# Opening the first MoE chunk half way through batch 0, and dividing attention outputs by the row sum instead of the probabilities

## The chip, the cores and the metric

The kernel runs on one core of a Trainium2 chip. The core has TensorE (PE in the profile: matmuls and transposes, with weight loads in a row of their own, PEld), VectorE (DVE), ScalarE (ACT), GpSimd (POOL) and SyncE (SP), which here only issues DMAs. Each engine works through its own list of instructions in a fixed order; a waiting instruction holds back everything behind it on that engine. The metric is the device time of the whole program in microseconds.

## The reference

Three stages in fp32, the output of each feeding the next. What matters here:

```
scores   s = scale * q_l k^T          # window of +-32 keys and 32 global keys; 4 batches x 8 heads x 512 queries, D = 64
p        e = exp(s - max(s));  p = e / (sum(e) + 1e-9)
out      o = p v                       # plus 32 global queries per batch that see all keys
x        = o of all heads side by side # 4 x 544 tokens, 512 wide
moe 1    h = x w_in;  g = max(h, 0) + alpha * min(h, 0);  x = g w_out      # w_in 512 x 2048, w_out 2048 x 512
moe 2    logits = x w_gate; every token goes to one of 8 experts of equal capacity; out = relu(x w1[e]) w2[e]
```

The weights of moe 1 and w_gate come as float64 and are decoded on the core.

## The kernel before

A tile scheduler writes the instruction lists: the kernel issues operations in an order of its own, and the scheduler, led by its own timeline, reorders them on each engine before the lists are fixed.

**Attention.** The work is cut into 16 units `u` = (batch, pair of heads), four to a batch, and each unit into two halves `j` of 256 queries (two blocks of 128). A *unit half* is the piece that the text counts in. For each, `scores` does four matmuls into PSUM, a fused mask-and-minimum on DVE (L376) and an exponential with row sums on ACT (L378); `norm` adds 1e-9 to the sums, takes the reciprocal (L384, L385) and multiplies the four 128x224 tiles of probabilities (L393 on DVE; with the flag `share` set, every second one on ACT, L391); `ptrans` transposes them on PE in two parts (L402), each copied to SBUF by ACT (L404); `pv` multiplies with v on PE (L413), and ACT copies the 128x256 result into `xb` (L414), the transposed activations of the batch. Per pair of units there is also a global part: `gscores` (L425, L427, L431), `gnorm`, `gtrans` (L450, L444) and `gpv` (L462), whose DVE copy (L465) fills the first 32 columns of `xb`. `gout` writes finished units to memory.

The generator `attention` runs the unit halves in the order (0,0), (0,1), (1,0), (1,1), ...: scores of number n, norm and transposes of n-1, pv of n-2. Loads are issued two units ahead (`load`, 736 KB of q and k, three buffers; `load_v`, 512 KB, four buffers).

**First stage, attention alone.** While `alone[0]` is set, PSUM is split among tags: `s` tiles have four banks, transposes two (`pX`), and everything else (`gs`, `gt`, `go`, `o`) shares the two banks of `pY`. The loop `while done[0] < UPB - 1` runs the generator until batch 0 has been written out, and decodes up to four parts of `w_in`. `decode` is one ACT operation (L78), four DVE operations on 128x512 (L79, L81, L82, L83), a cast on ACT (L67) and a subtraction on POOL (L68).

**Second stage, attention beside MoE.** Then a pool of four banks serves all attention tiles, and `gemm(c, 0)` starts: chunk `c` has 272 tokens, half a batch. `splitx` splits `xb` into a rounded part xh (ACT) and a rest xl (DVE L68, 128x1088). `gemm1` does twelve 128x272 matmuls (L167) for each of eight column blocks, DVE evaluates the activation from PSUM (L172, L186), ACT and POOL split it (`ghi`, `glo`), and the second product takes 96 matmuls (L200). A ratio of 0.9 shares turns between attention and MoE. The other twelve weight parts are decoded here, one per MoE step; `tc.issue_after(at_norm[UPB - 1, 1].ins)` puts their DVE work behind the last normalization of batch 0. `share` stays set until the parts are used up.

**Later stages.** Once attention is over, the second halves of `w_in` and `w_out` are decoded under the remaining chunks; then come the second half of moe 1, the router and the experts.

Of the kernel before, what the change touches and what calls it, by code (L numbers as in the profile page):

```python
# [15 lines left out]
OP = mybir.AluOpType  # L16
# [9 lines left out]
def tile_attention_moe_moe(ctx: ExitStack, tc: tile.TileContext, qkw, vw,  # L26
# [277 lines left out]
    with ExitStack() as at:  # L304
        mk = at.enter_context(tc.tile_pool(name="mk", bufs=1, side="right"))
        ld = at.enter_context(tc.tile_pool(name="ld", bufs=3, side="right"))
# [23 lines left out]
        NU = len(units)  # L330
        U = [dict() for _ in units]
# [14 lines left out]
        def load_v(u):  # L346
            d = U[u]
            vv = ld.tile([128, 2, NB, 2 * D], F32, name="vv", bufs=4)
            nc.sync.dma_start(out=vv.rearrange("p a i d -> p (a i d)"), in_=vw[u])
            d["va"], d["vb"] = vv[:, 0], vv[:96, 1]  # L350
# [5 lines left out]
        def scores(u, j):  # L356
            d = U[u]
            if j == 0:
# [4 lines left out]
                d["pr"] = pp.tile([128, 2, NB, KW], F32, name="pr")  # L363
                d["sm"] = pp.tile([128, 2, NB], F32, name="sm")
                d["mx"] = pp.tile([128, 2, NB], F32, name="mx")
# [5 lines left out]
            for ii in range(2):  # L371
                i = 2 * j + ii
                m = mask[:, 0 if i == 0 else 2 if i == NB - 1 else 1]
                for h in range(2):
                    sc = pp.tile([128, KW], F32, name="sc", bufs=4)
                    V.tensor_tensor_reduce(out=sc, in0=s[h][:, ii], in1=m, scale=-D ** -0.5, scalar=BIG,  # L376
                                           op0=OP.add, op1=OP.min, accum_out=d["mx"][:, h, i:i + 1])
                    A.activation(out=d["pr"][:, h, i], in_=sc, func=AF.Exp, bias=d["mx"][:, h, i:i + 1], scale=-1.0,  # L378
                                 accum_out=d["sm"][:, h, i:i + 1])

        def norm(u, j):
            d = U[u]
            sm = d["sm"][:, :, 2 * j:2 * j + 2]
            V.tensor_scalar(sm, sm, 1e-9, None, op0=OP.add)  # L384
            V.reciprocal(sm, sm)  # L385
            for ii in range(2):
                i = 2 * j + ii
                for h in range(2):
                    p, r = d["pr"][:, h, i], d["sm"][:, h, i:i + 1]
                    if h and share[0]:  # L390
                        A.mul(p, p, r)  # L391
                    else:
                        at_norm[u, j] = V.tensor_scalar(p, p, r, None, op0=OP.mult)  # L393

        def ptrans(u, j, half):
# [3 lines left out]
            for ii in range(2):  # L399
                for h in range(2):  # L400
                    p = d["pr"][:, h, 2 * j + ii]
# [4 lines left out]
        def pv(u, j):  # L406
            d = U[u]
            o = bank([128, 2, 128], "o")
# [5 lines left out]
            A.copy(d["x"][:, SG + 256 * j:SG + 256 * j + 256], o.rearrange("p i t -> p (i t)"))  # L414
# [61 lines left out]
        share, at_norm = [False], {}  # L476

        def attention():
# [7 lines left out]

            for n in range(2 * NU + 2):
                u, j = divmod(n, 2)
                if u < NU:
                    if j == 0 and u + 2 < NU:  # L490
                        load(u + 2)
                        load_v(u + 2)
                    scores(u, j)
                    yield 1.0
# [778 lines left out]
```

## Time and profile before

| | us |
|---|---|
| median of 3 runs | 901.78 (901.72 to 903.84) |
| profiled execution | 902.5 |
| its span | 900.7 |
| start of the first MoE matmul (L167) in the trace | 61.70 |

The profile is of one execution. A row of the page names line, engine, operation, the tile written and the tiles read, then how often it runs. Busy times are unions within a window; a matmul's own duration holds its pipeline latency, so what one costs in a stream is read from start to start. An fp32 matmul that is not a transpose leaves two records in the trace, a transpose or an fp32r matmul one. "PEclk" 1.00 means 2.4 GHz, 0.50 means 1.2 GHz.

### The profile page before, as it was taken

Reading aid. Unit: us, or ns where it says so; the run is one execution under the profiler, and the core shown is the slowest. Engines: PE = TensorE matmul, PEld = TensorE weight load, DVE = VectorE, ACT = ScalarE, POOL = GpSimd, SP = SyncE. Lnnn points to the kernel's source line nnn. Section 1 sums busy time; section 2 is a strip of 40 time slices with the busy share of each in tenths; the row PEclk is TensorE's granted clock in tenths of the full one; section 3 lists DMA queues with packets and bytes.
Section 4 is the critical chain, followed back from the end, with each engine's and each line's share of the span. In section 5 each row is a group of like instructions: output and inputs, shape, how many; then the busy total and the mean of one; then the engine's idle time right before and its main releaser. Section 6 shows DMA issues by size and latency. Waiting matters only on the chain.

```text
span 900.7 us, 18727 instructions
## 1 busy us (share of the span) xinstructions
PE 850.4 (94%) x7168; PEld 775.0 (86%) x7168; DVE 542.4 (60%) x1779; ACT 405.6 (45%) x949; POOL 426.3 (47%) x367
## 2 busy tenths in 40 slices
PE   6989999999998899999999999999899999899996
PEld 3677788888897899999999899999498998899995
DVE  5989946565639983355655756677475776621120
ACT  4977555564544452233333333331244444444531
POOL 1225311111106643355666865652567678778721
PEclk8989899999999999999999999999899999999998
DMA  8575414313035521022220215332455556456510
GB/s 294 174 251 174 130 60 152 96 63 125 32 113 157 169 82 63 25 68 95 67 84 1 76 49 168 118 119 72 119 155 169 158 168 187 145 169 183 169 44 36
DMA packets 50273, 107.66 MB, mean 120 GB/s; under 512 B 6728, under 2 KB 23112, under 8 KB 50184
## 3 DMA queue, kind: packets, MB, share of 16 engines
q1 hardware_dynamic: 47288, 97.56, 35.0%
q0 software_dynamic: 2896, 8.92, 2.7%
q8 instruction: 56, 0.92, 0.4%
q14 instruction: 33, 0.27, 0.1%
HBM read 88.63 MB, written 17.83 MB: 118 GB/s over the span
## 4 chain that ended last, share of the span: by engine, by line
PE 33%; DMA 8%; POOL 7%; issue 5%; ACT 3%; DVE 2%; POOLq 0%; ACTq 0%
PE h L1115 11%; PE h L167 10%; DMA raw<-in_moe_w_dram 7%; POOL m L68 6%; PE h L1005 3%; PE h L989 3%; PE lp L239 3%; ACT m L67 2%; POOL xg L940 1%; PE yt L228 1%; PE y L200 1%; PE pc L829 1%; POOL out_dram L1039 0%; DMA x2d<-yr 0%; PE pa L841 0%
## 5 line engine op out<-in xcount | busy, mean ns | idle before, releaser
L68 POOL TENSOR_TENSOR m<-raw,m 128x1024 fp32r<-128x1024 f32 x64 | 152.8, 2392 | 51.5 <-ACT m L67 51.1
L167 PE MATMUL h<-xh,win 128*128 128x272 f32 x768 | 165.5, 296 | 6.4 <-DVE g L186 5.7
L68 POOL TENSOR_TENSOR glo<-g,ghi 128x272 fp32r<-128x272 f32 x64 | 58.0, 909 | 179.3 <-ACT ghi L67 177.1
L167 PEld LDWEIGHTS h<-xh,win 128*128 128x128 f32 x768 | 126.1, 188 | 14.6 <-DVE g L186 7.5
L200 PE MATMUL y<-ghi,wout 128*128 128x272 f32 x512 | 113.0, 300 | 2.4 <-ACT ghi L67 2.0
L167 PE MATMUL h<-xl,win 128*128 128x272 f32 x384 | 111.3, 291 | 0.3 <-DVE xl L68 0.2
L1115 PE MATMUL h<-gr,wout 128*128 128x272 f32 x768 | 110.8, 295 | 0.4 <-POOL gr L68 0.4
L172 DVE TENSOR_SCALAR nm<-h,al 128x272 f32<-128x272 f32 x128 | 63.4, 496 | 77.0 <-PE h L167 76.2
L989 PE MATMUL h<-xsh,m 128*128 128x272 f32 x512 | 106.3, 297 | 1.1 <-ACT xsh L67 1.1
L67 ACT CAST m<-raw 128x1024 fp32r<-128x1024 f32 x64 | 66.9, 1049 | 82.0 <-DMA raw<-in_moe_w_dram 77.1
L1005 PE MATMUL h<-hh,m 128*128 128x272 f32 x512 | 103.4, 294 | 0.0
L1115 PEld LDWEIGHTS h<-gr,wout 128*128 128x128 f32 x768 | 99.3, 189 | 1.3 <-POOL gr L68 0.7
L200 PEld LDWEIGHTS y<-ghi,wout 128*128 128x128 f32 x512 | 84.8, 191 | 8.0 <-issue 4.0
L989 PEld LDWEIGHTS h<-xsh,m 128*128 128x128 f32 x512 | 83.2, 190 | 1.7 <-ACT xsh L67 1.4
L1005 PEld LDWEIGHTS h<-hh,m 128*128 128x128 f32 x512 | 81.5, 189 | 0.2
L200 PE MATMUL y<-glo,wout 128*128 128x272 f32 x256 | 75.3, 298 | 3.0 <-POOL glo L68 3.0
L1005 PE MATMUL h<-hl,m 128*128 128x272 f32 x256 | 75.7, 296 | 0.0
L989 PE MATMUL h<-xsl,m 128*128 128x272 f32 x256 | 75.2, 294 | 0.2 <-DVE xsl L68 0.2
L167 PEld LDWEIGHTS h<-xl,win 128*128 128x128 f32 x384 | 72.4, 189 | 1.6 <-DVE xl L68 0.7
L378 ACT ACTIVATE pr<-sc,mx 128x224 f32<-128x224 f32 x128 | 60.5, 475 | 23.5 <-DVE mx L376 23.2
L68 POOL TENSOR_TENSOR l<-gb,h 128x272 fp32r<-128x272 f32 x62 | 54.5, 893 | 22.9 <-ACT h L67 20.7
L68 POOL TENSOR_TENSOR gr<-gb,gr 128x272 fp32r<-128x272 f32 x64 | 47.9, 773 | 32.7 <-ACT gr L67 32.5
(233 smaller groups left out, 1737.4 us busy)
## 6 DMA issues: line engine op xcount, KB each, us to landing
raw<-in_moe_w_dram SPq DMA_DIRECT2D x64, 512.0 KB, 3.6
qk<-in_qk_dram SPq DMA_DIRECT2D x15, 736.0 KB, 6.6
vv<-in_v_dram SPq DMA_DIRECT2D x16, 512.0 KB, 5.5
raw<-in_moe_w_in_dram SPq DMA_DIRECT2D x16, 512.0 KB, 4.9
raw<-in_moe_w_out_dram SPq DMA_DIRECT2D x16, 512.0 KB, 3.6
xs<-xb SPq DMA_DIRECT2D x16, 272.0 KB, 4.5
xpart<-xd SPq DMA_DIRECT2D x32, 136.0 KB, 1.8
xb<-xs SPq DMA_DIRECT2D x8, 544.0 KB, 3.8
```

The lines of the kernel that those rows point to most:

```text
L67: a = A.copy(hi, src)
L68: return a, (lo_eng or V).tensor_tensor(lo, src, hi.bitcast(F32), op=OP.subtract)
L167: T.matmul(ps, wi[:, w, k, fs], x[:, k], start=i == 0, stop=i == 3 * KD - 1)
L172: V.tensor_scalar(nm, ps, 0.0, al[:, hf * KH + f:hf * KH + f + 1], op0=OP.min, op1=OP.mult)
L200: T.matmul(ps, wo[:, w, f, ds_], x[:, f], start=i == 0, stop=i == 3 * KH - 1)
L228: T.transpose(t[:, k * 128:(k + 1) * 128], tail["x"][:, k] if q == 2 else xo[:, k, a:b], ident)
L239: T.matmul(lp, w, x, start=first and i == 0, stop=last and i == 1)
L378: A.activation(out=d["pr"][:, h, i], in_=sc, func=AF.Exp, bias=d["mx"][:, h, i:i + 1], scale=-1.0, accum_out=d["sm"][:, h, i:i + 1])
L829: T.matmul(pc.rearrange("p a e -> p (a e)"), g[:, c:c + 2].rearrange("p a j -> p (a j)"), ohw[:, c:c + 2].rearrange("p a e -> p (a e)"), s ...
L989: T.matmul(ps, d["w1"][:, w, kk, fs], x[:, kk], start=i == 0, stop=i == 3 * KD - 1)
L1005: T.matmul(ps, d["w2"][:, w, f, ms], x[:, f], start=i == 0, stop=i == 3 * K3 - 1)
L1115: T.matmul(ps[j], wo[:, w, f, ds_], x, start=f == 0 and a == 0, stop=f == KH - 1 and a == 2)
```

## The change

- Batch 0 is done by halves: (0,0), (1,0), (2,0), (3,0), then (0,1), (1,1), (2,1), (3,1). Batches 1 to 3 keep the old order.
- Chunk 0 needs only the first 32 + 240 columns of `xb`. The first loop now ends after pv of (3,0), and `loadx(0, 0)` no longer waits for the whole batch.
- In batches 0 and 1 (`NBO = 2`) the probabilities are left undivided. `pv` spreads the reciprocal sums over the 64 output rows with four more matmuls against the identity into the second half of a 128x512 PSUM tile; ACT copies them to SBUF (`rs`), and DVE multiplies output by `rs` while it writes `xb`. ACT's old copy into `xb` is gone there. In batches 2 and 3 the division is as before, all of it on DVE; the flag `share` is gone.
- q/k buffers go from three to four. The first four units are loaded at once; later loads are issued when the third user of a buffer has been issued, four units ahead.
- Probabilities, sums and maxima have tiles per unit half.
- The remaining weight parts are put behind DVE's last multiply of the first halves of batch 0.

```diff
-        ld = at.enter_context(tc.tile_pool(name="ld", bufs=3, side="right"))
+        ld = at.enter_context(tc.tile_pool(name="ld", bufs=4, side="right"))
...
+        NBO = 2
...
+            d["pr", j] = pp.tile([128, 2, 2, KW], F32, name="pr", bufs=3)
+            d["sm", j] = pp.tile([128, 2, 2], F32, name="sm", bufs=4)
...
             V.tensor_scalar(sm, sm, 1e-9, None, op0=OP.add)
             V.reciprocal(sm, sm)
+            if units[u][0] < NBO:
+                return
             for ii in range(2):
-                i = 2 * j + ii
                 for h in range(2):
-                    p, r = d["pr"][:, h, i], d["sm"][:, h, i:i + 1]
-                    if h and share[0]:
-                        A.mul(p, p, r)
-                    else:
-                        at_norm[u, j] = V.tensor_scalar(p, p, r, None, op0=OP.mult)
+                    p = d["pr", j][:, h, ii]
+                    V.tensor_scalar(p, p, sm[:, h, ii:ii + 1], None, op0=OP.mult)
...
-            o = bank([128, 2, 128], "o")
+            late = units[u][0] < NBO
+            ot = bank([128, 2, 2, 128] if late else [128, 1, 2, 128], "o")
+            o = ot[:, 0]
+            if late:
+                for ii in range(2):
+                    for h, c in heads(u):
+                        T.matmul(ot[c, 1, ii], d["sm", j][:, h, ii:ii + 1].to_broadcast([128, D]), ident,
+                                 start=True, stop=True)
+                rs = tp.tile([128, 2, 128], F32, name="rs")
+                A.copy(rs, ot[:, 1])
...
-            A.copy(d["x"][:, SG + 256 * j:SG + 256 * j + 256], o.rearrange("p i t -> p (i t)"))
+            x = d["x"][:, SG + 256 * j:SG + 256 * j + 256].rearrange("p (i t) -> p i t", i=2)
+            if late:
+                at_norm[u, j] = V.tensor_tensor(x, o, rs, op=OP.mult)
+            else:
+                A.copy(x, o)
...
+            left[kind, u] = left.get((kind, u), 0) + 1
+            if left[kind, u] == 3 and u + 4 < NU:
+                (load if kind == "qk" else load_v)(u + 4)
...
+            seq = [(u, j) for j in range(2) for u in range(UPB)]
+            seq += [(u, j) for u in range(UPB, NU) for j in range(2)]
...
+                    if v == UPB - 1 and j2 == 0:
+                        quarter[0] = True
...
-        while done[0] < UPB - 1:
+        while not quarter[0]:
...
-            if want < NCH and (want, 0) not in X and done[0] >= (want // CPB + 1) * UPB - 1 and (
+            if want < NCH and (want, 0) not in X and (want == 0 or done[0] >= (want // CPB + 1) * UPB - 1) and (
...
-                        with tc.issue_after(at_norm[UPB - 1, 1].ins):
+                        with tc.issue_after(at_norm[UPB - 1, 0].ins):
```

PE around the opening, before: the last pv and the global pv of batch 0, one unit half of batch 1, then the first MoE matmuls (`h`).

```order
L402 MATMUL t<-ident,pr 128x128 x4
L413 MATMUL o<-pt,vv 64x128 x8
L402 MATMUL t<-ident,pr 96x128 x4
L462 MATMUL go<-gt,vv 64x32 x20
L413 MATMUL o<-pt,vv 64x128 x8
L370 MATMUL s<-qk 128x224 x4
L402 MATMUL t<-ident,pr 128x128 x4
L402 MATMUL t<-ident,pr 96x128 x4
L167 MATMUL h_803<-xh,win 128x272
L167 MATMUL h_855<-xh,win 128x272
L167 MATMUL h_803<-xl,win 128x272
```

PE around the opening, now (`o<-ident,sm` are the new matmuls that spread the reciprocal sums):

```order
L413 MATMUL o<-ident,sm 64x128 x8
L421 MATMUL o<-pt,vv 64x128 x16
L371 MATMUL s<-qk 128x224 x4
L401 MATMUL t<-ident,pr 128x128 x4
L401 MATMUL t<-ident,pr 96x128 x4
L167 MATMUL h_603<-xh,win 128x272
L167 MATMUL h_651<-xh,win 128x272
L413 MATMUL o<-ident,sm 64x128 x4
L371 MATMUL s<-qk 128x224 x4
L401 MATMUL t<-ident,pr 128x128 x3
L421 MATMUL o<-pt,vv 64x128 x6
L167 MATMUL h_603<-xl,win 128x272
```

Ahead of the first `h` now stand 28 score matmuls, 48 transposes, 32 pv matmuls and 16 of the new ones; before, 44, 80, 64 and none. The second halves of batch 0 follow behind and between `h`.

DVE ahead of the split of the first chunk (L68, `xl`), before:

```order
L384 TENSOR_SCALAR sm<-sm 128x2x2
L385 RECIPROCAL sm<-sm 128x2x2
L393 TENSOR_SCALAR pr<-pr,sm 128x224 x2
L79 TENSOR_SCALAR mag<-mag 128x512
L81 TENSOR_SCALAR mag<-mag 128x512
L82 SCALAR_TENSOR_TENSOR mag<-raw,mag 128x512
L465 COPY xb<-go 128x2x32
L83 SCALAR_TENSOR_TENSOR mag<-raw,mag 128x512
L79 TENSOR_SCALAR mag<-mag 128x512
L81 TENSOR_SCALAR mag<-mag 128x512
L68 TENSOR_TENSOR xl<-xb,xh 128x1088
```

DVE, now: the rows that end with the multiplies of the first halves of units 2 and 3 (L424); `xl` follows after two decode pairs and one unit half of masking (L377):

```order
L385 TENSOR_SCALAR sm<-sm 128x4
L83 SCALAR_TENSOR_TENSOR mag<-raw,mag 128x512
L386 RECIPROCAL sm<-sm 128x4
L424 TENSOR_TENSOR xb<-o,rs 128x256
L447 TENSOR_SCALAR gmx<-gmx 128x1
L448 RECIPROCAL gmx<-gmx 128x1
L385 TENSOR_SCALAR sm<-sm 128x4
L449 TENSOR_SCALAR gsc<-gsc,gmx 128x608
L386 RECIPROCAL sm<-sm 128x4
L457 COPY gt<-gt 96x128
L477 COPY xb<-go 128x2x32
L424 TENSOR_TENSOR xb<-o,rs 128x256 x2
```

The multiplications of probabilities (L393) are gone from this place, and four multiplies that read PSUM stand in DVE's list where ACT copied before. Ahead of `xl` DVE's list holds 28 masking operations instead of 44 and no multiplication of probabilities instead of 38; of the decode operations 6, 6, 5 and 4 (in the order L79, L81, L82, L83) instead of 8, 8, 7 and 7.

Further on, the stream of 48 matmuls of L200 that ends chunk 0's second product needs the last decoded part of `w_out`. Ahead of it PE's list holds, before: 64 score matmuls, 120 transposes, 104 pv, 142 `h`, 48 `y`. Now: 54, 96, 80, 144, 48, and 44 of the new ones. DVE's list of masking, decode and MoE operations up to the last decode holds 60 maskings before and 48 now.

SP's list of DMA issues from the start, before:

```order
L340 DMA qk<-in_qk_dram 128x960
L341 DMA qk<-in_qk_dram 128x512
L341 DMA qk<-in_qk_dram 128x1472
L349 DMA vv<-in_v_dram 128x1024 x2
L341 DMA qk<-in_qk_dram 128x1472
L349 DMA vv<-in_v_dram 128x1024 x2
L75 DMA raw<-in_moe_w_in_dram 128x1024 x3
L542 DMA al<-in_moe_alpha_dram 128x16x1
L543 DMA wg<-in_moe_w_gate_dram 128x4x8
L341 DMA qk<-in_qk_dram 128x1472
```

SP's list, now:

```order
L341 DMA qk<-in_qk_dram 128x960
L342 DMA qk<-in_qk_dram 128x512
L342 DMA qk<-in_qk_dram 128x1472
L350 DMA vv<-in_v_dram 128x1024
L342 DMA qk<-in_qk_dram 128x1472
L350 DMA vv<-in_v_dram 128x1024
L342 DMA qk<-in_qk_dram 128x1472
L350 DMA vv<-in_v_dram 128x1024 x2
L75 DMA raw<-in_moe_w_in_dram 128x1024 x3
L584 DMA al<-in_moe_alpha_dram 128x16x1
L585 DMA wg<-in_moe_w_gate_dram 128x4x8
L75 DMA raw<-in_moe_w_in_dram 128x1024
```

One more `qk` load of 736 KB stands ahead of the first `raw` (weights), and the fourth unit's q and k no longer stand behind the 128x4x8 load of the gate weights.

## Rows read from the trace of the kernel before

**Rows 1.** Page, part 1: busy time, share of the span and instructions of each engine

```profile
PE 850.4 (94%) x7168; PEld 775.0 (86%) x7168; DVE 542.4 (60%) x1779; ACT 405.6 (45%) x949; POOL 426.3 (47%) x367
```

**Rows 2.** Timeline of PE: the first MoE matmul

```profile
61.70 0.50 PE L167 MATMUL h<-xh,win 128*128 128x272 f32 x2
```

**Rows 3.** Windows by stage: length, busy us (instructions) per engine, PE clock, DMA share, GB/s

```profile
0.00:61.70 61.70, 47.90 (x403) 33.90 (x403) 48.96 (x188) 44.85 (x133) 12.84 (x25) 0.89 0.70 233
61.70:110.00 48.30, 45.17 (x356) 37.15 (x354) 47.00 (x133) 31.74 (x85) 22.61 (x18) 0.93 0.52 163
110.00:265.00 155.00, 155.00 (x1476) 136.41 (x1474) 85.68 (x332) 82.32 (x249) 19.77 (x24) 1.00 0.27 86
265.00:330.00 65.00, 56.90 (x421) 53.68 (x418) 60.31 (x97) 31.29 (x63) 35.28 (x30) 0.97 0.53 166
```

**Rows 4.** Windows of the first 117 us, by granted clock; columns as in rows 3

```profile
16.00:24.00 8.00, 6.16 (x36) 4.20 (x38) 6.12 (x27) 5.89 (x19) 1.32 (x1) 0.57 0.77 209
24.00:46.00 22.00, 19.04 (x179) 12.72 (x177) 21.55 (x84) 20.00 (x64) 4.19 (x3) 1.00 0.60 185
46.00:61.70 15.70, 13.62 (x146) 11.04 (x146) 13.36 (x38) 12.15 (x30) 3.40 (x3) 0.78 0.62 219
61.70:94.00 32.30, 29.26 (x233) 24.74 (x230) 32.27 (x91) 22.15 (x59) 15.09 (x13) 1.00 0.54 178
94.00:102.00 8.00, 7.91 (x71) 6.26 (x71) 8.00 (x18) 4.81 (x14) 4.81 (x3) 0.58 0.70 190
```

**Rows 5.** Waits of PE, 0 to 62: who, for whom, us, times, longest

```profile
PE s L370 <- DMA qk<-in_qk_dram: 4.5, 1, 4.5
PE s L370 <- DVE mx L376: 2.7, 2, 2.5
```

**Rows 6.** Waits of PE, 61.7 to 117

```profile
PE h L167 <- DVE g L186: 2.8, 2, 1.5
```

**Rows 7.** Timeline of PE from 117.0: start, us, operation, records; a next start ends one

```profile
117.00 0.29 PE L200 MATMUL y<-ghi,wout 128*128 128x272 f32 x1
...
122.92 0.29 PE L200 MATMUL y<-ghi,wout 128*128 128x272 f32 x1
123.13 1.10 PE L413 MATMUL o<-pt,vv 128*64 128x128 f32 x16
124.16 1.03 PE L370 MATMUL s<-qk 64*128 64x224 f32 x8
125.12 0.66 PE L402 MATMUL t<-ident,pr 128*128 128x128 f32 x4
125.53 0.38 PE L167 MATMUL h<-xl,win 128*128 128x272 f32 x1
```

**Rows 8.** Lines of DVE, 0 to 110: shapes, count | busy us, mean ns

```profile
L393 DVE TENSOR_SCALAR pr<-pr,sm 128x224 f32<-128x224 f32 x56 | 20.9, 430 | 0.1
L376 DVE CUSTOM_DVE_ANT_0 sc<-s,mask 128x224 f32<-128x224 f32 x60 | 20.9, 379 | 6.9 <-PE s L370 6.5 <-ACT pr L378 0.2
L82 DVE SCALAR_TENSOR_TENSOR mag<-raw,mag 128x512 int32<-128x512 int32 x16 | 13.2, 827 | 0.1
L83 DVE SCALAR_TENSOR_TENSOR mag<-raw,mag 128x512 int32<-128x512 int32 x16 | 11.9, 741 | 0.0
L81 DVE TENSOR_SCALAR mag<-mag 128x512 int32<-128x512 int32 x16 | 8.8, 558 | 0.1
L79 DVE TENSOR_SCALAR mag<-mag 128x512 f32<-128x512 f32 x16 | 7.6, 479 | 1.8 <-ACT mag L78 1.8
```

**Rows 9.** Lines of DVE by form, whole span: an add with one PSUM operand

```profile
L1128 DVE TENSOR_TENSOR pt<-h,pt 128x272 f32<-128x272 f32 x28 | 12.0, 437 | 3.8 <-PE h L1115 2.3 <-issue 0.4 <-ACT m L67 0.3
```

**Rows 10.** Windows, 8 to 16: columns as in rows 3

```profile
8.00:16.00 8.00, 5.55 (x33) 3.15 (x32) 6.60 (x34) 4.44 (x16) 0.00 (x0) 1.00 1.02 412
```

**Rows 11.** Timeline of ACT from 16: start, us, operation [idle before, releaser]

```profile
16.91 0.66 ACT L78 ACTIVATE mag<-raw 128x512 f32<-128x512 f32 x1 [1.89 <-DMA raw<-in_moe_w_in_dram]
```

**Rows 12.** Source view of line 393: duration ns least/median/most

```profile
L393 DVE TENSOR_SCALAR pr<-pr,sm x124: 321/331/1417, 9.5 to 253.8; 128x224 f32<-128x224 f32 x124
```

More of the change, by code (lines that the diff above doesn't have):

```diff
@@ L347, in load_v @@
             d = U[u]
-            vv = ld.tile([128, 2, NB, 2 * D], F32, name="vv", bufs=4)
+            vv = ld.tile([128, 2, NB, 2 * D], F32, name="vv")
             nc.sync.dma_start(out=vv.rearrange("p a i d -> p (a i d)"), in_=vw[u])
@@ L475, in tile_attention_moe_moe, with free, gs_, gp_ @@
         done = [-1]
-        share, at_norm = [False], {}
+        at_norm = {}
+        left = {}
+        quarter = [False]
+        def free(kind, u, j):
+            if u >= NU:
+                return
+            left[kind, u] = left.get((kind, u), 0) + 1
+            if left[kind, u] == 3 and u + 4 < NU:
+                (load if kind == "qk" else load_v)(u + 4)
+        def gs_(p):
+            gscores(p, 0)
+            gscores(p, 1)
+            free("qk", 2 * p, 2)
+            free("qk", 2 * p + 1, 2)
+        def gp_(p):
+            gpv(p)
+            free("vv", 2 * p, 2)
+            free("vv", 2 * p + 1, 2)
         def attention():
@@ L485, in one @@
                     yield x
+            seq = [(u, j) for j in range(2) for u in range(UPB)]
+            seq += [(u, j) for u in range(UPB, NU) for j in range(2)]
             for n in range(2 * NU + 2):
[L488 to L492, printed above, removed]
+                if n < 2 * NU:
+                    u, j = seq[n]
                     scores(u, j)
+                    free("qk", u, j)
                     yield 1.0
                 if 1 <= n <= 2 * NU:
-                    a_ = divmod(n - 1, 2)
-                    norm(*a_)
-                    ptrans(*a_, 0)
+                    norm(*seq[n - 1])
+                    ptrans(*seq[n - 1], 0)
                     yield 0.45
-                    ptrans(*a_, 1)
+                    ptrans(*seq[n - 1], 1)
                     yield 0.45
                 yield from one()
+                if alone[0]:
+                    yield from one()
                 if n >= 2:
-                    pv(*divmod(n - 2, 2))
+                    v, j2 = seq[n - 2]
+                    pv(v, j2)
+                    free("vv", v, j2)
                     yield 1.0
-                    v, j2 = divmod(n - 2, 2)
+                    if v == UPB - 1 and j2 == 0:
+                        quarter[0] = True
+                        yield 0.1
                     if v % 2 and j2:
@@ L517, in tile_attention_moe_moe @@
         load_v(0)
+        load(2)
         load_v(1)
+        load(3)
+        load_v(2)
+        load_v(3)
         mask = mk.tile([128, 3, KW], F32, name="mask")
@@ L545, in tile_attention_moe_moe @@
         alone[0] = False
-        share[0] = True
         first.close()
```

24 lines of the change are left out of this document (10 added, 14 removed).

## The prediction

> **What bounds the kernel now.** I read the busy line first, then windows by stage, then the stretch that the change touches by clock and by waits. TensorE is busy 850.4 of 900.7 us [rows 1], so the time is PE's work plus what PE loses. The first MoE matmul starts at 61.70 [rows 2]. The stage windows show where PE loses: 13.8 us without work up to 61.7 (61.70 - 47.90), 3.1 from there to 110, none from 110 to 265 (155.00 of 155.00), 8.1 from 265 to 330 [rows 3]. By clock: from 16 to 24 and from 46 to 61.7 the granted clock is 0.57 and 0.78, and again 0.58 from 94 to 102 [rows 4]; matmuls at 1.2 GHz take twice as long, so a stretch of 8 us at 0.58 (16% of it at the upper level) has 6.7 us at 1.2 GHz and loses half of that, 3.4. Before 61.7 the largest waits are for the first load (4.5, not avoidable) and for DVE's masking (2.7) [rows 5]; after it, 2.8 us for DVE's activation of the MoE chunk [rows 6]. In both stretches DVE is the full engine: 21.55 of 22.00 us from 24 to 46, 32.27 of 32.30 from 61.7 to 94, while PE has room [rows 4]. So up to 110 DVE, busy 47.00 of the last 48.30 us, sets the pace; from 110 to 265 PE does, and DVE there is at 85.68 of 155 [rows 3].
>
> **What the change adds.** Sixteen unit halves (batches 0 and 1) get four more matmuls each, 64 in all, of the form 128x64 by 128x128, which is that of pv. Sixteen records of pv (eight matmuls) take 1.03 us from start to start (123.13 to 124.16), 0.129 each [rows 7]: 64 x 0.129 = 8.2 us. Going from MoE to attention costs a little: the last `y` starts at 122.92 and pv at 123.13, 0.21 where 48 matmuls from 117.00 took (122.92 - 117.00) / 47 = 0.126 each, so 0.09 a change [rows 7]; a dozen changes more, an estimate, are 1.0. Nothing hides this where PE is full. Batch 1's half of it falls mostly into such a stretch; batch 0's is counted here too and its cover in the next terms. Bounds: 8.2, if the new groups always stand beside pv, and 16.5 if the two column halves did not run side by side as pv's do; I take 9.2, since the form is the same.
>
> On ACT the copy of `rs` replaces the copy into `xb`, same size, and four divisions go: nothing. On DVE 60 divisions go over the whole run and 16 multiplies with one PSUM operand come, 128x256; the nearest row is an add with one PSUM operand on 128x272, 0.437 us [rows 9]. Loads, stores and weights are as many as before; four units' q, k and v are issued ahead of the weights. One q/k load more, 736 KB at 412 GB/s [rows 10], puts the first weights back by 1.8 us, from 16.91 [rows 11] to about 18.7. That counts, because DVE and ACT have the first decode in their lists after three unit halves and wait there. Later loads are issued up to four units ahead, which I cost at nothing; a late one would cost no more than the 4.5 us of the first [rows 5].
>
> **What opening early gives.** At the first `h`, PE's list has done 16 score matmuls, 32 transposes and 32 pv less, and 16 new ones more. A group of 4 score matmuls takes 0.96 (124.16 to 125.12), four transposes 0.41 [rows 7]: 16 x 0.24 + 32 x 0.103 + 32 x 0.129 - 16 x 0.129 = 3.8 + 3.3 + 4.1 - 2.1 = 9.1 us of work less. So each microsecond by which the opening comes before 61.7 - 9.1 = 52.6 is lost time saved.
>
> When does it open? DVE was busy 48.96 us up to 61.7 [rows 3]. Ahead of the split of the chunk its list now lacks 38 divisions at 20.9 / 56 = 0.37, 16 maskings at 20.9 / 60 = 0.35, and 2 + 2 + 2 + 3 decode operations at 0.48, 0.55, 0.83 and 0.74 [rows 8]: 14.1 + 5.6 + 5.9 = 25.6; four multiplies add 1.7. That leaves 25.1. DVE starts at 6.5, the idle time before its first masking [rows 8]. It reaches the first decode after 12 maskings and some small work (12 x 0.35 + 2 for the global part), waits until 18.7 + 0.66 for ACT's first decode step [rows 11], and has about 19 us left: 38.4. With no other wait the opening is at 39, the lower end. The upper end keeps PE's present share: 47.90 busy in the 57.2 us from 4.5 on; 47.90 - 9.1 = 38.8 busy at that share is 46.4, so 51. I take 43, a third of the way up: in the nearest row, 24 to 46, DVE is full and PE busy 19.04 of 22 [rows 4], so the pace is DVE's, but the output tiles of the first stage pass through two PSUM banks, with PE, ACT and DVE taking turns, and that costs some microseconds. Saved: 52.6 - 43 = 9.6 (13.6 to 1.6).
>
> **The stretch after it.** From 61.7 to 117.0, where the stream of 48 `y` starts [rows 7], PE now loses 2.8 us in waits for DVE [rows 6] and 3.4 at the lower clock, which follows the idle time just before 94 [rows 4]: 6.2. In the new kernel DVE does this stretch without divisions (18 of the 56), with 20 maskings against 16, but with 9 more decode operations moved in from ahead of the opening. So DVE is about as full as it was, and PE has more to do beside it (28 new matmuls, a fuller MoE). PE is then nearer to being the bound, and a late DVE finds other matmuls in PE's list. I take half of the loss, 3.1, as gone; the ends are 0 and 6.2.
>
> After that PE has no idle time until attention ends [rows 3], so what was gained is kept. The window 265 to 330, 8.1 us idle and DVE busy 60.31 of 65 [rows 3], is the decode of the second half of the weights. The MoE has then run beside 28 unit halves instead of 24 and is a little under one chunk further; the chunks that are left still outlast the decode, so this wait stays, neither better nor worse.
>
> **The sum** on the span: +9.2 - 9.6 - 3.1 = -3.5, so 897.2. The profiled execution took 902.5, 1.8 above its span, and 0.7 above the median of 901.78: 901.8 - 3.5 = 898.3.
>
> **A rule that speaks against it.** A division lasts 0.331 us at the median and up to 1.417 [rows 12]; the mean of the first 110 us is 0.430 [rows 8], 0.1 more than undisturbed, 5.5 us over 56. In my sum that goes with the divisions. The Trainium skill (SBUF — State Buffer, section Who interferes with whom) says that DVE and GpSimd share one pair of ports, that scalar operations in the two-port mode and operations with two SBUF inputs compete for it with GpSimd, and that the loser is blocked for the whole instruction. The trace has the spread, but does not say who held the ports. By that rule the delay is GpSimd's to hand out and not the division's own: its subtractions for the weights stay, and the decode operations next in DVE's list would take it. The rule makes a rival of its own, the second below.
>
> **Rivals.** First, DVE's list flows: opening at 39 and no loss behind it. That is 4 us and 3.1 us better, 891. For it speaks that DVE's sum is the smaller one; against it that in the trace no stage of this kind ran without handover losses.
>
> Second, GpSimd's blocking moves to the decode (L81, L82), which already average 0.558 and 0.827 [rows 8]. Then DVE keeps about half of 38 x 0.1 ahead of the opening, 2 us, and the stretch behind it gains nothing: 898.3 + 2 + 3.1 = 903.4, no change.
>
> Third, slower: the output tile waits for DVE. Before, ACT emptied it as soon as pv was done; now it waits its turn in DVE's list, and ahead of the four multiplies stand decode operations of 0.83 and 0.74 [rows 8] and maskings. While the tile waits, one of two banks is held, and the next global scores, their transposes or the next output queue behind it on PE, and everything of PE behind those. At one decode pair (1.6) for four tiles ahead of the opening and half of that for the other four of batch 0, it costs 6.4 + 3.2 = 9.6: 908. It decides from an opening later than 46.5, where the rest gives nothing. For it speaks that ACT was the less loaded one, 22.15 of 32.30 against DVE's 32.27 [rows 4]; against it that later there are four banks and other matmuls between.
>
> That the change would not do what it says is ruled out by the lists, which have `h` after 28 score matmuls.
>
> **Chances.** My forecast 45% (893 to 903 by itself), first rival 17%, second 20%, third 18%. Within 0.3%, 899.1 to 904.5, a measurement of this kernel can't tell from no change. Of the forecast's 45, 27 are faster, 16 the same, 2 slower; the first rival's 17 are faster; of the second, 2 faster, 13 the same, 5 slower; of the third, 1 faster, 2 the same, 15 slower. So 47% faster, 31% the same, 22% slower. The range leaves out a tenth at each side: 890.5 to 907.
>
> **What would show it.** The first `h` near 43 and no earlier than 39; the new matmuls at 0.26 a pair; the first decode step of ACT near 18.7 with a wait for DMA before it; DVE's multiplies near 0.43; PE full from shortly after the opening, with the waits for DVE and the stretch at 0.58 shorter or gone; 110 to the end of attention still without idle time. An opening after 47, or PE waits for L424, make the prediction wrong towards slower; waits of the MoE for L82 or L83, towards no change.

## The result, and the profile after

The changed kernel takes 907.94 us (median of 20 runs, 904.13 to 913.12), the kernel before 902.05 (20 runs, 899.77 to 907.55): a ratio of 1.0059, with a 95% interval of 1.0042 to 1.0077. It is slower by about 5.9 us, where 898.3 was forecast. A second measurement of both (e12 below) gave 1.0065 (1.0042 to 1.0088).

The busy line of the page, against [rows 1]: TensorE has 128 matmul records more (the 64 new matmuls, two records each) and 10.2 us more of busy time; VectorE has 12 us less.

```profile
PE 860.6 (95%) x7296; PEld 783.1 (86%) x7296; DVE 530.4 (58%) x1735; ACT 404.9 (45%) x945; POOL 421.9 (46%) x367
```

The first MoE matmul, against 61.70 in [rows 2], in the timeline of PE:

```profile
48.20 0.52 PE L167 MATMUL h<-xh,win 128*128 128x272 f32 x2
```

So the opening did come early, by 13.5 us. The stage windows, against [rows 3], in the same columns (length, busy us and instructions of PE, PEld, DVE, ACT, POOL, then PE clock, DMA share, GB/s):

```profile
0.00:61.70 61.70, 48.31 (x416) 37.12 (x418) 38.89 (x140) 38.61 (x110) 13.63 (x26) 0.86 0.64 222
61.70:110.00 48.30, 45.97 (x352) 36.97 (x347) 43.96 (x117) 31.85 (x85) 18.38 (x16) 0.96 0.49 159
110.00:265.00 155.00, 155.00 (x1473) 134.76 (x1472) 81.99 (x326) 81.49 (x248) 21.25 (x26) 1.00 0.28 90
265.00:330.00 65.00, 61.06 (x519) 56.15 (x518) 50.14 (x100) 30.23 (x67) 24.41 (x22) 1.00 0.42 129
```

Up to 61.70 VectorE was relieved by 10.07 us, but TensorE is busy there for as long as before, 48.31 us against 47.90. The only window in which TensorE's idle time clearly fell is the last, 3.94 us against 8.10, and that is the one the prediction said would stay. The finer windows, against [rows 4]:

```profile
16.00:24.00 8.00, 5.06 (x34) 3.47 (x33) 5.40 (x23) 6.21 (x19) 0.08 (x1) 0.87 0.63 175
24.00:46.00 22.00, 18.23 (x201) 15.16 (x203) 12.08 (x41) 13.50 (x36) 5.44 (x4) 0.66 0.45 164
46.00:61.70 15.70, 15.13 (x136) 12.34 (x132) 15.02 (x42) 10.88 (x30) 4.18 (x4) 1.00 0.63 212
61.70:94.00 32.30, 29.97 (x227) 23.98 (x222) 32.13 (x81) 21.99 (x56) 14.57 (x13) 0.95 0.66 212
```

From 24 to 46 no engine is full any more: VectorE is busy 12.08 of 22 us, ScalarE 13.50, and TensorE 18.23, at a granted clock of 0.66 (a mix of its 1.2 and 2.4 GHz levels). From 46 on VectorE is full again, 15.02 of 15.70 and 32.13 of 32.30. What VectorE lost in divisions it lost where it then had nothing to do; behind the opening it is as full as before. The timeline of PE from 20 us on (idle time and its releaser in brackets) shows work that waits for other work:

```profile
20.42 1.33 PE L371 MATMUL s<-qk 64*128 64x224 f32 x8 [2.67 <-DVE mx L377]
...
23.91 2.35 PE L474 MATMUL go<-gt,vv 128*64 128x32 f32 x40
26.06 1.10 PE L413 MATMUL o<-ident,sm 128*64 128x128 f32 x8
28.69 1.98 PE L437 MATMUL gs<-qk 128*64 128x512 f32 x4 [1.53 <-DVE xb L477]
30.46 1.88 PE L421 MATMUL o<-pt,vv 128*64 128x128 f32 x16
```

The pv group (L421, x16) takes 1.88 us there and 1.10 in [rows 7]. The wait of 2.67 goes back to the first weights: VectorE's next operation was a step of their decode (L79), which waited for ScalarE's first step (L78), and that one for the weights to land:

```profile
18.60 0.43 DVE L79 TENSOR_SCALAR mag<-mag 128x512 f32<-128x512 f32 x1 [2.76 <-ACT mag L78]
17.91 0.66 ACT L78 ACTIVATE mag<-raw 128x512 f32<-128x512 f32 x1 [1.46 <-DMA raw<-in_moe_w_in_dram]
```

### The profile page after: what moved, and what is told of

Same layout as the page of the kernel before. It is cut to its first block, busy times and chain, and to the rows that moved or that the text cites. A ratio compares the mean times of both kernels' runs of the same rounds, so it can differ in the third digit from the quotient of the medians.

```text
span 908.2 us, 18931 instructions
## 1 busy us (share of the span) xinstructions
PE 860.6 (95%) x7296; PEld 783.1 (86%) x7296; DVE 530.4 (58%) x1735; ACT 404.9 (45%) x945; POOL 421.9 (46%) x367
## 4 chain that ended last, share of the span: by engine, by line
PE 57%; DMA 11%; DVE 10%; issue 9%; POOL 8%; ACT 4%; SPq 1%; POOLq 0%; ACTq 0%; DVEq 0%
PE h L167 17%; PE h L1154 11%; DMA raw<-in_moe_w_dram 9%; PE y L200 8%; POOL m L68 6%; PE o L421 3%; PE s L371 3%; PE lp L239 3%; PE t L401 2%; PE h L1028 2%; DVE mag L82 2%; ACT m L67 2%; DMA raw<-in_moe_w_in_dram 2%; POOL xg L979 2%; PE h L1044 1%
## 5 line engine op out<-in xcount | busy, mean ns | idle before, releaser
L68 POOL TENSOR_TENSOR m<-raw,m 128x1024 fp32r<-128x1024 f32 x64 | 152.7, 2391 | 54.0 <-ACT m L67 53.0
L167 PE MATMUL h<-xh,win 128*128 128x272 f32 x768 | 168.4, 299 | 4.1 <-DVE g L186 3.7
L167 PEld LDWEIGHTS h<-xh,win 128*128 128x128 f32 x768 | 127.3, 190 | 13.8 <-DVE g L186 5.9
L68 POOL TENSOR_TENSOR glo<-g,ghi 128x272 fp32r<-128x272 f32 x64 | 56.4, 884 | 170.5 <-ACT ghi L67 168.0
L200 PE MATMUL y<-ghi,wout 128*128 128x272 f32 x512 | 113.0, 299 | 0.4 <-ACT ghi L67 0.3
L200 PEld LDWEIGHTS y<-ghi,wout 128*128 128x128 f32 x512 | 83.9, 189 | 6.5 <-issue 4.2
L200 PE MATMUL y<-glo,wout 128*128 128x272 f32 x256 | 74.6, 295 | 0.0
L68 POOL TENSOR_TENSOR l<-gb,h 128x272 fp32r<-128x272 f32 x62 | 54.5, 893 | 23.0 <-ACT h L67 20.7
L68 POOL TENSOR_TENSOR gr<-gb,gr 128x272 fp32r<-128x272 f32 x64 | 47.9, 773 | 32.9 <-ACT gr L67 32.8
```

The source lines that it names most:

```text
L68: return a, (lo_eng or V).tensor_tensor(lo, src, hi.bitcast(F32), op=OP.subtract)
L167: T.matmul(ps, wi[:, w, k, fs], x[:, k], start=i == 0, stop=i == 3 * KD - 1)
L200: T.matmul(ps, wo[:, w, f, ds_], x[:, f], start=i == 0, stop=i == 3 * KH - 1)
```

## The experiments

All are measured against the kernel before on the same chip; its median there was 901.65 to 903.15, so ratios are compared, not times, and a range in brackets behind a ratio or a difference is a 95% interval. The lines of code are shortened. Theory A was formed from the profile above: the 64 matmuls cost their full price, and the opening came late because TensorE ran a chain of dependent work at 1.2 GHz. Theory B: VectorE's work sets the pace. Theory C: the two PSUM banks that hold the outputs do.

**Each half of the change alone.** e1 keeps order and opening, e2 scales batch 0 only, e3 keeps only the scaling.

```
e1:  NBO = 2  ->  NBO = 0
e2:  NBO = 2  ->  NBO = 1
e3:  seq = [(u, j) for u in range(NU) for j in range(2)]
     while not quarter[0]  ->  while done[0] < UPB - 1   (the chunk's condition and the global parts' turns as before)
```

> The new order and the early opening stay; the outputs are no longer scaled: in both batches the probabilities are divided on VectorE as before, so the 64 matmuls that spread one over the row sum, their ScalarE copies and the 16 multiplies of the outputs are gone. Theory A (the change pays for the added matmuls on TensorE, and the opening came late because TensorE ran its chain of dependent work at 1.2 GHz): the 64 matmuls go at 0.129 us each, 8.2 us, and the chain to the first MoE matmul loses a link, so 899.5 us (897 to 902), first MoE matmul at 46 to 47.5. Theory B (VectorE is what the new opening is short of): 24 more divisions of 0.43 us lie ahead of the opening, it comes later than 50, and batch 1's 32 come back beside the MoE chunk: 905 us or more.

> Outputs are scaled in batch 0 only; batch 1 is divided on VectorE as before. Theory A: 32 matmuls fewer at 0.129 us, 4.1 us, all after the opening: 903.8 us (902.5 to 905.5), the first MoE matmul unchanged at 48.2. Theory B: batch 1's 32 pairs of divisions, 64 of 0.43 us less 8 multiplies of 0.42 us, 24 us of VectorE, delay TensorE in the stretch of the first chunks: not faster than 907.

> The old order and the old opening after the whole of batch 0; only the scaling of the outputs of batches 0 and 1 stays. Theory A: the added 64 matmuls lie on TensorE's path and VectorE's relief gives back at most the 7.2 us of waits of the first stage: 906 us (902 to 910). Theory B: VectorE set the pace of the first stage, and its 27.5 us less of divisions bring the old opening forward by 5 us or more: 900 us or less.

e1: 908.62, ratio 1.0063 (1.0037 to 1.0088). Theory A missed by 9 us; B was right on the opening, at 53.26, with VectorE full in 24:46:

```profile
24.00:46.00 22.00, 17.06 (x165) 12.68 (x165) 21.10 (x61) 14.13 (x38) 7.60 (x5) 0.66 0.51 163
```

So opening early without the scaling costs 5.7 us (3.3 to 7.9), as much as the whole change.

e2: 906.51, 1.0030 (1.0005 to 1.0054), between the two. (Theory B's 24 us for it count batch 1's 32 divisions twice; by the same working they are 10.4.) e3: 909.80, 1.0077 (1.0051 to 1.0103), as A said: the scaling alone costs 7.0 us (4.6 to 9.3), and VectorE's relief does not bring the old opening forward, which comes at 61.24. But the two halves together cost no more than either, so they aren't independent. e1 also lacks ScalarE's share of the divisions; that was only 4 of 128 in the kernel before, and e13 tries a larger one.

**The stall and the clock.** e4 queues the first decode on ScalarE behind unit 3's exponentials; e6 loads the first weights ahead of two units' values; e7 does e4's edit in the kernel before; e17 fills TensorE's wait with repeated transposes. (e7, and e15 and e16 below, also put the split of the gate weights behind a later exponential.)

```
e4:  with tc.issue_after(last_exp[UPB - 1, 0].ins): f(dc, 0, i)
e6:  load_v(2), load_v(3) issued behind the first and the second part
e7:  with tc.issue_after(last_exp[0].ins): f(dc, 0, i)     (kernel before)
e17: for _ in range(3): T.transpose(t[:, ii, h], ..., ident)   (unit 1, first half pair)
```

> The changed kernel with one thing altered: on ScalarE the first weights' decode is queued behind unit 3's exponentials, so that ScalarE and VectorE no longer stand still until the first weights have landed (1.46 and 2.76 us), and TensorE not behind them (2.67 us). Theory A (the idle time at 17.8 to 20.4 is what lets the clock fall to 1.2 GHz, and the chain runs at that clock until the opening): PEclk in 24:46 rises from 0.66 to over 0.9, the first MoE matmul comes at 42 to 44 in place of 48.2, and the time is 903 us (901 to 905). Theory C (the two output banks held by VectorE's copies and multiplies set the pace, not the clock): the first MoE matmul stays later than 46.5 and the time within 1.5 us of 907.9.

> The changed kernel with the values of units 2 and 3 loaded behind the first and the second part of the raw first weights, in place of ahead of both: the weights land some 2.6 us earlier, by the 18 us at 400 GB/s that the opening loads take, and ScalarE, VectorE and TensorE wait less behind them. Theory A (the idle time near 18 to 20 lets the clock fall, and the fall delays the opening): PEclk in 24:46 over 0.85, first MoE matmul at 44 to 46, 905 us (903.5 to 906.5), as with the later decode. Theory C (the chain through the two output banks sets the pace): first MoE matmul later than 47 and 907 us or more.

> The kernel before with the first weights' decode queued on ScalarE behind later exponentials (and the gate weights' split behind batch 0's), so that ScalarE (1.89 us) and VectorE (1.43 us) no longer stand still for the first weights. Theory A carried over (the stall and the low clock behind it, 0.57 in 16:24, hold up the kernel before as well): first MoE matmul 2 to 4 us ahead of 61.7, 900 us (898.5 to 902). Rival E (in the old order VectorE's work ahead of the opening, 39.60 us busy of 46, sets it, so the stall's idle time is used anyway): within 1 us of 903.

> The changed kernel with unit 1's transposes of the first half pair issued three times into the same place, 16 more on TensorE where it then waits 2.67 us for VectorE (17.75 to 20.42): the idle time is filled with work that changes nothing, no other engine's work alters. Theory A (that idle time lets the clock fall for the stretch behind it): PEclk in 24:46 at 0.85 or more (0.66 and 0.81 in the two profiles of the changed kernel), first MoE matmul at 44 to 45.5, mean clock of the runs above 0.984 (0.981 to 0.983), 905.8 us (904.5 to 907). Rival: the clock falls anyway behind the waits at 27 to 38 us, and the time stays within 1 us of 907.7.

e4: 905.65, 1.0035 (1.0011 to 1.0059), clock 0.86 in 24:46, opening at 45.88, both short of what A wanted, and the opening earlier than C allowed; against the changed kernel it is 2.2 us (-0.5 to 4.9) faster by the ratios. e6: 907.83, 1.0056 (1.0034 to 1.0078): opening at 45.88 as well, at a clock of 0.78, and no gain. e7: 903.41, 1.0008 (0.9989 to 1.0028): the opening came at 58.77 (61.70 and, in e11, 59.41 without the edit), and the time did not move, as rival E had it. e17: 909.36, 1.0076 (1.0052 to 1.0100), slower than both of its theories said; the wait was filled in part only (0.92 us were left, and 1.92 for ScalarE's copy came instead), and its clock in 24:46 was 0.76:

```profile
24.00:46.00 22.00, 20.67 (x232) 15.73 (x231) 14.37 (x49) 15.46 (x39) 5.19 (x4) 0.76 0.46 164
```

In none of these does an opening 2 to 3 us earlier give a gain that its interval shows. And over whole runs of one measurement (e12's) the mean granted clock is higher in the changed kernel, 0.9829 in 9 runs, than in the kernel before, 0.9789 in 18. So the changed kernel isn't slower because it is granted less clock; that half of theory A falls.

**The price of the 64 matmuls, and the banks.** e5 issues each twice; e10 empties the output bank by ScalarE and multiplies the copy.

```
e5:   for _ in range(2): T.matmul(ot[c, 1, ii], d["sm", j]..., ident, ...)
e10:  A.copy(x, o); at_norm[u, j] = V.tensor_tensor(x, x, rs, op=OP.mult)
```

> The changed kernel with each of the 64 matmuls that spread one over the row sum issued twice into the same place, the second writing what the first wrote: it prices them alone. Theory A (they lie on TensorE's path at full price): 64 more at 0.129 us, 8.2 us, so 916 us (914 to 918). Rival D (half of them fall into TensorE's waits of the first 110 us and cost nothing there): 912 us or less.

> The changed kernel with the output bank freed by a copy on ScalarE (0.36 us), and VectorE multiplying the copy in SBUF in place of the bank. Theory C (the two output banks, held until VectorE comes round to the multiply, set the pace ahead of the opening): first MoE matmul at 45 to 47 and 905.5 us (904 to 907). Theory A (the waits for the multiply are 0.4 us in the trace, and ScalarE has 16 more copies): 908 us (907 to 910).

e5: 908.49, 1.0062 (1.0039 to 1.0085), the same as the changed kernel's. 64 matmuls more cost 0.3 us (-2.3 to 2.9), not 8.2, as rival D had it. The matmuls are there: 256 records against 128 in the source view of their line, with the same duration:

```profile
L414 PE MATMUL o<-ident,sm x256: 272/273/472, 25.3 to 158.8; 128*64 128x128 f32 x128
```

e10: 906.77, 1.0059 (1.0037 to 1.0080). The time lies in C's range, but the changed kernel took 907.56 (1.0065) in the same measurement, so the gain is 0.5 us (-2.3 to 3.4), and the opening, at 47.21, lies between those of the changed kernel's two profiles (48.20 and 45.16 in e12). The banks aren't shown to be the pace either.

**The opening alone, and two repeats.** e9 keeps order and scaling and opens as before; e11 and e12 are the two kernels once more.

```
e9:  while not quarter[0]  ->  while done[0] < UPB - 1   (new seq kept, NBO = 2)
```

> The changed kernel with its new order of the half pairs and its scaling, but the first chunk opened as before, after the whole of batch 0 (and the first wout parts behind the last multiply of batch 0). Theory F (the early opening itself is worth something, and it is the order ahead of it that spends this: fewer independent instructions for TensorE between 16 and 46 us): first MoE matmul at 61 to 66 and 913 us (910 to 916). Rival G (the opening's place is worth nothing, since the sum of TensorE's waits stays the same wherever it lies): within 2 us of 907.9.

> The kernel before, unaltered, for a second profile. If the stretch from the end of the first half's output matmuls to the end of the program, the same instructions in the same order in all these kernels, varies by itself (512.4 to 517.8 us in the ten profiles so far, 512.4 in the one of before), it comes out nearer to 514.7 here, and the first part nearer to 386.5 than to 388.3. If before's 512.4 belongs to the kernel, it comes again within 1 us.

> The changed kernel, unaltered, for a second profile and time. If the 1.2 GHz stretch ahead of the opening (PEclk 0.66 in 24:46, first MoE matmul at 48.20) belongs to the kernel, PEclk in 24:46 is 0.60 to 0.72 again and the opening within 1 us; if it varies with the execution (0.78 and 46.20 in the kernel scaled in batch 0 alone, which has the same instructions up to there), PEclk differs by more than 0.08. The stretch after the first half's output matmuls, 516.4 in the first profile: 513 to 516. Time 907.5 us (906 to 909).

e9: 911.94, 1.0120 (1.0087 to 1.0153), beside 907.56 for e12: opening early is worth 4.4 us with this order, 5.0 (1.3 to 8.6) by the ratios. The time was right, the opening was not: with the whole of batch 0 ahead of it, it came at 55.01, so some 7 to 10 us of earlier opening are priced here.

```profile
55.01 0.40 PE L167 MATMUL h<-xh,win 128*128 128x272 f32 x1
```

Against e3, which has the old order and the old opening (61.24), the new order costs 3.9 us (0.1 to 7.7) by the ratios. e12, the changed kernel's second profile, opened at 45.16 with a clock of 0.81 in 24:46, so the 3 us by which the first one opened later belong to that execution:

```profile
24.00:46.00 22.00, 18.24 (x227) 14.26 (x227) 14.40 (x48) 15.55 (x40) 5.19 (x4) 0.81 0.47 166
```

e11 opened at 59.41. The stretch from the last `y` (L200) of the first half to the end, whose matmul records are the same in the same order in all 20 profiles (but for some 60 of 4,072 at its start), took 512.4 us in the first profile of before and 515.1 in the second, 516.4 and 513.2 for the changed kernel, and 511.8 to 517.8 over all. So half of the 7.5 us between the first two spans lies in this stretch, within its spread from execution to execution.

**Divisions shared with another engine, without the new matmuls.** e13 divides as before, the second head's on ScalarE; e14 on GpSimd; e15, e8, e16 and e18 put edits together.

```
e13: NBO = 0; if h and units[u][0] < 2: A.mul(p, p, sm[:, h, ii:ii + 1])
e14: NBO = 0; if h and units[u][0] < 2: P.tensor_scalar(p, p, sm[:, h, ii:ii + 1], ...)
e15: e13 with e4's edit              e8:  NBO = 1 with e4's edit
e16: e8 with e13's A.mul              e18: e13, unit 0's second transposes four times
```

> The later decode and the scaling in batch 0 only, together, on the changed kernel. By their own measured gains (907.9 to 905.65, and to 906.5) they add up to 904.2. Theory A at its full price of 4.1 us for 32 matmuls: 901.5 (900 to 903), which would put it ahead of the kernel before. Theory B (batch 1's divisions hold up the first chunks on VectorE): 904 to 906.

> The new order and the early opening with the outputs not scaled: the probabilities are divided as before, the second head's in batches 0 and 1 on ScalarE (the kernel before did so too while it decoded weights behind the opening), the rest on VectorE. Against the opening alone (908.6 us, first MoE matmul at 53.26, VectorE busy 21.10 of 22 us in 24:46) VectorE loses half of its divisions. Theory F (the early opening is worth some 5 us, the 64 matmuls cost 7, and VectorE's divisions were what the opening alone was short of): first MoE matmul at 45 to 48 and 902.5 us (900.5 to 904.5). Rival H (ScalarE, busy 14.13 of 22 us there, becomes the pace with 2 divisions more per half pair): opening later than 50, 906 us or more.

> As the run before, with the second head's divisions of batches 0 and 1 on GpSimd in place of ScalarE. Theory F: GpSimd is busy 7.60 of 22 us in 24:46 of the opening alone, has room for 2 divisions per half pair, and the opening comes at 45 to 48: 902.5 us (900.5 to 904.5). Rival I (GpSimd's divisions take over 1 us each beside VectorE's and hold up the transposes, or the weights' low parts behind them): opening later than 50, 906 us or more.

> The divisions shared with ScalarE as in the run before last, and the first weights' decode queued on ScalarE behind unit 3's exponentials (and the gate weights' split behind later ones), which took 2.1 us off the changed kernel. Theory F: 900.5 us (898.5 to 902.5), below the kernel before. Rival H: 904 or more.

> The later decode, the scaling in batch 0 only, and in batch 1 the second head's divisions on ScalarE: the version at 903.5 us with half of batch 1's divisions taken from VectorE. Theory B, in part (batch 1's divisions on VectorE hold up the first chunks: VectorE is busy 32.23 of 32.30 us in 61.7:94 there): 902 us (900.5 to 903.5). If VectorE is not what TensorE waits for there (0.5 to 2.4 us of TensorE's idle time in 46:110): within 1 us of 903.5.

> The version with the divisions shared with ScalarE (901.05 us), and unit 0's transposes of the second 96 columns of the first half pair issued four times, 12 more, ahead of the wait at 13.3 to 14.9 us behind which its clock fell (PEclk 0.50 in 16:24). Theory A: PEclk in 16:24 over 0.8, first MoE matmul 1 to 3 us ahead of 50.11, mean clock of the runs above 0.978 (0.976), 899.5 us (898 to 901). Rival (TensorE is not what the opening waits for there: VectorE is busy 19.58 of 22 us in 24:46): within 1 us of 901.

e13: 901.05, 0.9988 (0.9965 to 1.0011), 6.4 us (3.8 to 9.0) under the changed kernel by the ratios, although it opens at 50.11, later than any profile of that one:

```profile
50.11 0.49 PE L167 MATMUL h<-xh,win 128*128 128x272 f32 x2
```

Its windows show the place of VectorE's work: the divisions fit into 24:46, where the changed kernel leaves VectorE idle for 9.92 us.

```profile
24.00:46.00 22.00, 16.91 (x183) 13.59 (x179) 19.58 (x56) 17.47 (x46) 7.75 (x6) 0.73 0.61 195
```

So the time was right and the opening expected for it wrong. Against e1, whose 32 divisions more are on VectorE, it is 6.8 us (3.7 to 9.9) faster: in the new order VectorE's divisions cost about what the scaling costs, and e13 pays neither. It is also the cleanest price of order and early opening together: 1.1 us (-1.0 to 3.2) faster than the kernel before.

e14: 911.22, 1.0086 (1.0057 to 1.0115), as rival I had it. A division takes 0.872 us on GpSimd, 0.331 on VectorE [rows 12] and 0.476 on ScalarE, and the opening falls to 56.35:

```profile
L393 POOL TENSOR_SCALAR pr<-pr,sm x32: 837/872/1283, 9.7 to 142.0; 128x224 f32<-128x224 f32 x32
```

The Trainium skill (GPSIMD Engine Reference, Engine selection) calls GpSimd about twice as slow as VectorE with two inputs and near line rate with one; here one input and a scalar per partition took 2.6 times as long. For this shape the measurement decides; how much of it is a fixed cost of an instruction, no run here shows.

e8: 903.53, 1.0009 (0.9985 to 1.0034), between its two theories. e15: 902.00, 0.9992 (0.9970 to 1.0014). e16: 902.06, 0.9995 (0.9971 to 1.0018), as theory B had it, which shows nothing by itself, since the rival's range overlaps. e18: 902.26, 0.9987 (0.9965 to 1.0008), e13's ratio. In e18 the clock in 16:24 rose from 0.50 to 1.00 and the opening came at 47.85, as theory A has it, and the time stayed. All four are faster than the changed kernel by more than their intervals (e8, the least, by 4.5 us, 1.8 to 7.2). None beats the kernel before by more than its interval; e13 and e18 are 1.1 us ahead at the middle.

## Why the prediction was wrong, step by step

I take TensorE's time apart with the traces: work is the number of records times a rate at full clock, and all else up to a point is lost (waits, low clock, changes of work). The rates are 0.126 a MoE matmul, 1.03 for 16 records of pv or of the new matmuls, 0.96 for 8 of scores, 0.103 a transpose [rows 7]; from starts in the same trace 0.228 and 0.066 for the two forms of global scores (512 and 96 columns), 0.031 for global pv and 0.1 for the small ones of the weights. No attention record is missing up to the last `y`, so work is off only by the rates; differences between kernels depend little on them. Each column is one stretch, in us, work / lost:

```
                   opening  up to it      to the last pv   to the last y
before               61.7   32.9 / 28.8   179.0 / 24.4     107.8 / 15.3
before again (e11)   59.4   32.9 / 26.5   179.0 / 25.2     107.8 / 15.3
after                48.2   23.7 / 24.5   210.8 / 29.3      92.7 / 10.8
after again (e12)    45.2   23.7 / 21.5   210.8 / 29.1      92.7 / 10.8
e3 scaling alone     61.2   36.0 / 25.2   184.2 / 23.4     107.8 / 16.1
e1 opening alone     53.3   21.6 / 31.6   204.6 / 29.9      92.7 / 12.0
e13 on ScalarE       50.1   21.6 / 28.5   204.6 / 25.6      92.7 / 11.8
e9 late opening      55.0   30.0 / 25.0   190.2 / 25.2     107.8 / 17.6
e5 spread twice      47.0   25.8 / 21.2   217.0 / 25.9      92.7 / 10.9
```

- **What the change adds, +9.2.** Work up to the last `y` grows by 7.5 us: the 64 matmuls are 8.2 at the rate forecast, and six MoE matmuls less stand ahead of that point. In the old order the scaling costs about that, 7.0 in e3. In the new order it costs nothing against divisions on VectorE (e1) and 6.4 against divisions shared with ScalarE (e13). Its price isn't the matmul count either. In e5 the second 64 added 8.2 us of work, the measured time stayed, and in its one profile the last `y` came 3.4 us later than in the mean of the two above. Of these 64, 36 more stand ahead of 110 us and 28 behind. Up to 110 the lost time is 32.3 us in e5 and 39.6 and 36.7 in the changed kernel, so there they filled time that was lost anyway; from 110 to the last pv it is 14.8 against 14.2 and 13.9, so there they were paid. "Nothing hides this where PE is full" holds from 110 us on only.
- **What opening early gives, -9.6: the step that failed most.** The work done less at the opening was right, 9.2 for 9.1. The opening at 43 became 48.2 and 45.2, inside the bounds of 39 and 51, and the lost time up to it fell by 4.6 (means of the two profiles), half of 9.6. "The pace is DVE's" failed: VectorE was idle for 9.92 of 22 us from 24 to 46 (7.60 in e12), and PE, ACT and DVE waited for each other. PE's idle time up to the opening was 13.8 and 12.2 us before and is 12.8 in both profiles now, so the waits moved and did not shrink. e9 and e12 price the early opening at 4.4 us, and the new order, for which the sum has no term, costs 3.9 (e9 against e3). Which of the waits sets the opening stays open: later decode, weights first, filled waits and freed banks (e4, e6, e17, e10) each gave less than their interval.
- **The stretch after it, -3.1: failed too.** From the opening to the last pv the lost time rose by 4.4 us, and from there to the last `y` it fell by 4.5. The border between the two moves: attention now ends 22 us later. Over both, the lost time is 39.7 and 40.5 before and 40.1 and 39.9 after: nothing was gained where 3.1 was forecast. The prediction counted 6.2 us lost from 61.7 to 117; the table's count has 12.3 from 61.7 to 110 alone, and now 15.1 from 48.2 to 110. VectorE is as full as it was up to 94 us, which may be why PE can go no faster there; that is argued, not tested. PE also changes more often between MoE and attention up to the last pv, 236 times against 194, where I put a dozen more; 42 at the 0.09 of [rows 7] would be 3.8. But e2, with 210 changes, loses 30.6 there, and e13, with 230, only 25.6, so this count doesn't explain the loss. Nor does the scaling: e1 has none and loses 29.9. What sets it the runs don't show.
- **"What was gained is kept" and "this wait stays", 0.** PE waits less beside the second decode (3.94 for 8.10 us, windows above), since fewer chunks are left there. This comes with the early opening: the fifteen profiles of kernels that open after batch 0's first halves lose 10.6 to 12.6 us from the last pv to the last `y`, and the five of those that wait for the whole of batch 0, e9 with the new order among them, 15.3 to 17.6. It is no gain by itself, as the stretch ahead of it loses as much more.
- **The sum.** Predicted were -12.7 lost and +9.2 added; the table has -4.8 lost, nearly all of it ahead of the opening, and +7.5 added: 2.7 slower at the last `y` (387.6 to 390.2, means). The mean spans of the runs in e12's measurement differ by 4.9 us; the 2 us between lie in the spread of two profiles each, and stay open. e13 prices the two gains without the scaling, with shared divisions: 1.1 us (-1.0 to 3.2), where 12.7 was forecast.

Of the rivals, the third had the sign and the time, 908, by luck and not by its mechanism: PE waited 0.4 us for L424 in all, and e10 freed the bank with no gain beyond its interval. The second is partly seen: L82 rose from 0.827 [rows 8] to 0.984, L83 fell from 0.741 to 0.699, and the four decode steps together rose from 41.5 to 43.7 us, 2.2 in all, the size of its 2 us, and the stretch behind the opening gained nothing, as it said. But no run shows that GpSimd is the cause, and its time, 903.4, was 4.5 us short.

```profile
L82 DVE SCALAR_TENSOR_TENSOR mag<-raw,mag 128x512 int32<-128x512 int32 x16 | 15.7, 984 | 0.2
L83 DVE SCALAR_TENSOR_TENSOR mag<-raw,mag 128x512 int32<-128x512 int32 x16 | 11.2, 699 | 0.1
L81 DVE TENSOR_SCALAR mag<-mag 128x512 int32<-128x512 int32 x16 | 9.7, 610 | 0.1
L79 DVE TENSOR_SCALAR mag<-mag 128x512 f32<-128x512 f32 x16 | 7.1, 450 | 2.9 <-ACT mag L78 2.8
```

Small steps that held: ACT's first decode came later behind a DMA wait, at 17.91 (18.7 forecast), the multiplies took 0.424 (0.43 forecast), and PE has no idle time from 110 to 265.

```profile
L424 DVE TENSOR_TENSOR xb<-o,rs x16: 384/424/425, 32.4 to 162.6; 128x256 f32<-128x256 f32 x16
```

## What to carry to other kernels

An earlier start of the next stage is worth only the lost time that it removes over the whole program: split work from lost time in each stage, and add the stages up, because a border that moves shifts losses from one to the next. Ask which engine is full in the stage that the work moves into. Taking work from a full engine helps until the next wait takes its place: here all of VectorE's divisions were taken away, it then stood idle for 9.92 of the 22 us from 24 to 46, and TensorE paid for it; with half of those divisions on ScalarE instead and the other half where it was, the program took no longer than before (e13). Before a few us are read out of two profiles, compare a stretch in which nothing was altered: here it differed by 4 us between the first two.

## What the runs showed of the hardware

- 64 more matmuls of the shape of pv, issued right behind their twins, cost 0.3 us (-2.3 to 2.9) where their own rate makes 8.2; 36 of them stand in a stretch where TensorE loses time anyway (e5).
- The clock of one stretch varies from execution to execution of one kernel: 0.66 and 0.81 in 24:46 of the changed kernel, and with it the opening, by 3.0 us.
- One multiply by a scalar per partition, 128x224: 0.331 us on VectorE, 0.476 on ScalarE, 0.872 on GpSimd.
